# Reordering an attention-plus-feed-forward kernel: sink scores one pair later, one more x tile transposed by DMA

## The chip, the cores and the metric

The kernel runs on one core of a Trainium2 chip. The metric is the device time of one execution in microseconds (us); of several runs the median is taken. Before the change it is 197.56 us, the median of 8 runs between 197.08 and 198.56.

## What is computed

The reference takes q, k and v of 4 batches, 8 heads, 768 positions and 64 values per head, and five feed-forward inputs. First it does attention with a window and sinks:

```
scores = q @ k.T / sqrt(64)
keep   = (key position < 4) or (0 <= query position - key position < 128)
a      = softmax(where(keep, scores, -1e9))
attn   = a @ v
```

The heads of a position are laid side by side, which gives x with 3072 rows and 512 columns. Then comes a multiplicative feed-forward:

```
a = x @ w1        # 512 -> 1024
b = x @ w2        # 512 -> 1024
h = (a * b) @ w3  # 1024 -> 1024
out = h @ w_out   # 1024 -> 512
```

All inputs and the output are float32.

## The kernel before

**Tiles.** A batch b has three tiles t of 256 positions, and four pairs r of heads. The names of the plan (line 526 on) are steps of TensorE work, and each is one generator in the code:

- `t3.i.j` and `fm.i.n` fold w3 and w_out into one matrix `w3o` = w3 @ w_out: `t3` transposes a block of 128 rows of w3 (`fold_w3`), `fm` multiplies it with 128 columns of w_out (`fold_mm`). Blocks 0, 1 and 2 of w3 come as float32 on SyncE's (SP's) queue, in two halves; the other five come as bf16 on GpSimd's (POOL's) queue.
- `tpk`/`tpq.b.t` transpose k and q on TensorE. For the tiles in `XPOSE` the same is done by a DMA transpose from SP (`transposes_dma`, line 270).
- `sc.b.r.t` are the scores of a pair in a tile, then an exponential on ScalarE and the mask on VectorE (`scores`). One of them per batch or tile also makes the sink scores: four matmuls into the tile `sp` (line 303) and one exponential into `es`.
- `av.b.r.t` multiplies the weights with v and divides by their sum on VectorE (`values`); the result is the bf16 tile `xn`. `sv.b` makes the sink values.
- `xt.b.r.t` transposes x of two pairs on TensorE and copies it from PSUM to `xT` (`x_transposes`, line 360). For the tiles in `X_XPOSE` two DMA transposes from SP do this for a tile (`x_transposes_dma`, line 370), one for each 128 positions.
- `g.b.c.dt.half` is one half of a gate: half 0 is x @ w1 for 128 of the 1024 columns and chunk c of tokens, copied by ScalarE to `a_sb`; half 1 is x @ w2, multiplied with `a_sb` by VectorE into `ab`. Batch 0 has three chunks of 256 tokens; the others have two of 384. So g.2.1 needs x of tiles 1 and 2.
- `p.b.m` is the projection of 128 tokens with `w3o`, eight matmuls of 512 columns, copied out of PSUM and stored from SP.

**Order.** Nothing is scheduled at run time. The long loop at the end of the kernel plays the program through with estimated durations. It takes TensorE's work strictly in the order of `PLAN`. For the other engines (ScalarE, VectorE, SP) it puts each ready instruction in their order as the estimates say, so constants such as `LAG`, `SW_BEGIN`, the additions to `arrive`, `XX_US` and `XP_US` decide how SP's transposes and stores stand, which of ScalarE and VectorE copies out of PSUM, and where idle matmuls (`keep_busy`, tile `pz`) are put in a planned gap. On the chip every engine works through its own fixed list and waits for semaphores.

**Queues.** POOL issues the loads, with a cast from float32 to bf16, in the order of the list `order`; eight are in flight. SP issues the three float32 blocks of w3, then all DMA transposes and the stores, in one list, and a DMA of SP also waits until the one eight places before it has landed. PSUM has four buffers `mm` and two `sc`.

Of the kernel before, what the change touches and what calls it, by code (L numbers as in the profile page):

```python
# [21 lines left out]
def kernel(  # L22
# [29 lines left out]

    CHUNKS = [[(256 * i, 256 * i + 256) for i in range(3)]] + [[(0, 384), (384, 768)]] * (B - 1)
    XPOSE = [(1, 2), (2, 0), (2, 1), (2, 2), (3, 0), (3, 1), (3, 2)]
    X_XPOSE = [(2, 0), (2, 1), (2, 2), (3, 0), (3, 1), (3, 2)]
    CUTS = (0, 128, 256, 384, 512)
    HALVED = 8
    PIECES = ((0, 256), (256, 384), (384, 512))
# [1 line left out]
    SPLIT = (0, 1)  # L60
    RAW = (('w3', 0), ('w3', 1), ('w3', 2))
# [62 lines left out]
    def load(what, *i):  # L124
# [18 lines left out]
        else:  # L143
# [2 lines left out]


    RAW_US = 0.6
    order = [("w3", 5), ("wo", 128, 256), ("wo", 384, 512), ("w3", 4), ("wo", 0, 128), ("k", 0, 0), ("q", 0, 0),
             ("w3", 3), ("k", 0, 1), ("wo", 256, 384), ("v", 0, 0), ("q", 0, 1), ("w3", 7), ("w3",  # L150
             6), ("w2", 256, 512), ("q", 0, 2), ("v", 0, 1), ("w1", 256, 512), ("k", 0, 2), ("w2",
             768, 1024), ("w1", 768, 1024), ("w2", 512, 768), ("w1", 512, 768), ("w2", 0, 256),
             ("w1", 0, 256), ("v", 0, 2)] + [
             ("qkv", b, 0, 6) for b in range(1, B)]

    nc.scalar.preload_act_table_set("natural_log_exp_and_others")
# [302 lines left out]


    arrive = {}
    LAG, RATE, BEGIN, SW_BEGIN = (0.9, 2.5), 0.383, 2.0, 2.6

    def pieces(what, *i):
        if what == "qkv":
# [15 lines left out]
        else:  # L481
            yield 1.03 * (i[1] - i[0]) / 512, 1024, [(what, n) for n in range(i[0] // P, i[1] // P)]

    streams = [[[0.8 + RAW_US * n + 1.2, {"w3": 0.475, "wo": 1.03 * (CUTS[x[1] + 1] - CUTS[x[1]]) / 256 if x[0] == "wo" else 0}.get(x[0], 0.555),
                 {"w3": 4096, "wo": 4 * (CUTS[x[1] + 1] - CUTS[x[1]]) if x[0] == "wo" else 0}.get(x[0], 512), [("raw",) + x]] for n, x in enumerate(RAW)],
               [[None, mb, size, keys] for x in order for mb, size, keys in pieces(*x)]]
    at, issue, landed, heads_ = BEGIN, 1.3, [], [0, 0]
    STEP = 0.05
    issued = 0

    def issue_more():
        nonlocal issue, issued
        while issued < len(streams[1]) and (issued < 8 or len(landed) > issued - 8):
            if issued >= 8:
                issue = max(issue, landed[issued - 8])
            issue += {2: 0.6, 6: 1.25, 8: 0.9}.get(issued, 0.0)
            streams[1][issued][0] = max(SW_BEGIN, issue + 1.3)
            issue += 0.57 if streams[1][issued][2] == 4096 else 0.9
            issued += 1

    issue_more()
    while any(h < len(s) for h, s in zip(heads_, streams)):
        live = [n for n in (0, 1) if heads_[n] < len(streams[n])
                and streams[n][heads_[n]][0] is not None and streams[n][heads_[n]][0] <= at]
        total = sum(streams[n][heads_[n]][2] for n in live)
        for n in live:
            x = streams[n][heads_[n]]
            x[1] -= RATE * STEP * x[2] / total
            if x[1] <= 1e-9:
                heads_[n] += 1  # L510
                for key in x[3]:
                    arrive[key] = at + STEP + LAG[n] + (0.5 if at > 20.0 else 0.0)
                if n == 1:
                    landed.append(at + STEP + LAG[n])
                    issue_more()
        at += STEP

    for key in arrive:
        if key[0] in ("k", "q", "v"):
            arrive[key] += (0.0, 0.3, -0.5, 2.0)[key[1]]  # L520

    tasks = {}
    SP_US = 0.7
    XP_US, XX_US, LATE_US = (0.0, 9.0, 8.7, 7.8), (9.0, 9.0, 9.0, 7.7, 6.0, 3.6, 3.6, 3.6, 3.6), 12.0
    PLAN = """
        t3.0.0 t3.2.4 t3.0.4 t3.5.0 t3.2.0 t3.1.0 t3.1.4 fm.5.1 fm.2.1 fm.0.1 fm.1.1 fm.5.3 fm.0.3
        t3.4.0 fm.1.3 fm.2.3 fm.2.0 fm.0.0 fm.5.0 fm.4.0 fm.4.1 fm.1.0 tpk.0.0.2 tpq.0.0.0 tpk.0.0.0
        tpq.0.0.2 fm.4.3 t3.3.0 sc.0.0.0 sc.0.1.0 tpk.0.1.2 tpk.0.1.0 fm.3.0 fm.3.3 fm.1.2 fm.0.2 fm.3.2
        fm.5.2 sv.0 sc.0.2.0 av.0.0.0 av.0.1.0 fm.3.1 fm.2.2 sc.0.3.0 tpq.0.1.2 tpq.0.1.0 fm.4.2 t3.7.0
        xt.0.0.0 av.0.2.0 sc.0.0.1 sc.0.1.1 av.0.3.0 t3.6.0 fm.7.0 fm.7.1 fm.7.2 xt.0.2.0 fm.6.3 fm.7.3  # L530
        sc.0.2.1 sc.0.3.1 tpq.0.2.2 fm.6.1 av.0.0.1 av.0.1.1 fm.6.0 g.0.0.2.0 g.0.0.3.0 fm.6.2 tpk.0.2.0
        tpq.0.2.0 tpk.0.2.2 g.0.0.2.1 av.0.2.1 av.0.3.1 xt.0.0.1 sc.0.0.2 sc.0.1.2 g.0.0.6.0 g.0.0.7.0
        xt.0.2.1 g.0.0.7.1 g.0.0.6.1 g.0.0.3.1 g.0.1.7.0 g.0.1.7.1 g.0.0.4.0 sc.0.2.2 sc.0.3.2 g.0.0.4.1
        g.0.1.0.0 g.0.1.4.0 g.0.1.2.0 g.0.1.0.1 av.0.0.2 g.0.1.4.1 g.0.0.5.0 g.0.0.1.0 g.0.0.1.1
        g.0.1.2.1 g.0.0.5.1 av.0.1.2 g.0.1.5.0 g.0.0.0.0 tpk.1.0 xt.0.0.2 g.0.1.5.1 tpq.1.0 av.0.2.2
        g.0.0.0.1 g.0.1.3.0 av.0.3.2 sc.1.0.0 sc.1.1.0 sv.1 g.0.1.3.1 g.0.1.6.0 g.0.1.1.0 g.0.1.6.1
        tpk.1.1 g.0.1.1.1 xt.0.2.2 sc.1.2.0 sc.1.3.0 av.1.0.0 tpq.1.1 p.0.0 g.0.2.7.0 g.0.2.2.0 av.1.1.0
        g.0.2.6.0 g.0.2.6.1 sc.1.0.1 sc.1.1.1 av.1.2.0 av.1.3.0 g.0.2.2.1 g.0.2.7.1 p.0.1 g.0.2.0.0
        g.0.2.0.1 sc.1.2.1 sc.1.3.1 xt.1.2.0 g.0.2.5.0 g.0.2.1.0 g.0.2.5.1 av.1.0.1 g.0.2.3.0 av.1.1.1
        g.0.2.1.1 g.0.2.4.0 g.0.2.4.1 p.0.2 g.0.2.3.1 av.1.2.1 av.1.3.1 xt.1.0.0 p.0.3 xt.1.2.1 xt.1.0.1  # L540
        sc.1.0.2 sc.1.1.2 p.0.4 g.1.0.2.0 g.1.0.4.0 sc.1.2.2 sc.1.3.2 g.1.0.2.1 g.1.0.3.0 av.1.0.2
        g.1.0.5.0 g.1.0.4.1 av.1.1.2 g.1.0.7.0 av.1.2.2 g.1.0.5.1 av.1.3.2 g.1.0.7.1 g.1.0.3.1 g.1.0.6.0
        xt.1.0.2 xt.1.2.2 g.1.0.1.0 sc.2.0.0 sc.2.1.0 g.1.0.6.1 g.1.1.2.0 g.1.1.7.0 g.1.0.1.1 g.1.1.5.0
        g.1.1.7.1 g.1.1.2.1 av.2.0.0 sc.2.2.0 sc.2.3.0 av.2.1.0 g.1.1.5.1 g.1.1.4.0 g.1.1.4.1 g.1.1.1.0
        av.2.2.0 g.1.1.1.1 g.1.1.6.0 g.1.1.6.1 g.1.1.3.0 g.1.0.0.0 g.1.1.0.0 av.2.3.0 sc.2.0.1 sc.2.1.1
        g.1.1.3.1 sv.2 p.0.5 g.1.1.0.1 g.1.0.0.1 sc.2.2.1 sc.2.3.1 av.2.0.1 p.1.4 av.2.1.1 sc.2.0.2
        sc.2.1.2 av.2.2.1 av.2.3.1 p.1.5 sc.2.2.2 sc.2.3.2 p.1.3 av.2.0.2 av.2.1.2 sc.3.0.0 sc.3.1.0
        av.2.2.2 p.1.2 p.1.0 av.2.3.2 sc.3.2.0 sc.3.3.0 p.1.1 g.2.0.1.0 g.2.0.7.0 g.2.0.2.0 av.3.0.0
        g.2.0.1.1 g.2.0.7.1 g.2.0.2.1 av.3.1.0 g.2.0.5.0 g.2.0.4.0 g.2.0.5.1 g.2.0.0.0 g.2.0.0.1
        g.2.1.4.0 av.3.2.0 g.2.0.4.1 g.2.1.0.0 g.2.1.3.0 g.2.1.4.1 g.2.1.3.1 g.2.1.5.0 g.2.1.0.1  # L550
        g.2.1.1.0 g.2.0.3.0 sv.3 g.2.1.5.1 av.3.3.0 g.2.1.2.0 sc.3.0.1 sc.3.1.1 g.2.0.3.1 g.2.1.1.1
        g.2.0.6.0 g.2.0.6.1 g.2.1.2.1 g.2.1.6.0 sc.3.2.1 sc.3.3.1 av.3.0.1 av.3.1.1 p.2.0 sc.3.0.2
        sc.3.1.2 av.3.2.1 av.3.3.1 p.2.2 g.2.1.7.0 sc.3.2.2 sc.3.3.2 g.2.1.7.1 av.3.0.2 g.2.1.6.1 p.2.1
        av.3.1.2 p.2.5 av.3.2.2 p.2.3 g.3.0.6.0 g.3.0.5.0 av.3.3.2 g.3.0.1.0 g.3.0.5.1 g.3.0.6.1
        g.3.0.4.0 g.3.0.1.1 g.3.0.4.1 g.3.0.2.0 g.3.0.3.0 g.3.0.0.0 g.3.0.0.1 g.3.0.2.1 p.2.4 g.3.1.6.0
        g.3.1.6.1 g.3.0.3.1 g.3.1.7.0 g.3.1.2.0 g.3.1.0.0 g.3.1.2.1 g.3.1.7.1 g.3.1.0.1 g.3.1.4.0
        g.3.1.3.0 g.3.1.1.0 g.3.1.4.1 g.3.0.7.0 g.3.0.7.1 g.3.1.1.1 g.3.1.3.1 p.3.0 g.3.1.5.0 g.3.1.5.1
        p.3.1 p.3.2 p.3.4 p.3.3 p.3.5
    """

    def task(name, prio, gen, stages, after=(), loads=(), ring=None, started=(),
# [25 lines left out]
    for i in range(KFF):  # L587
        t3 = []
# [16 lines left out]
    def xn_free(b, t):  # L605
        b, t = (b, t - 2) if t == 2 else (b - 1, t + 1)
        return [] if b < 0 else ([("xd", b, t, i) for i in range(2)] if (b, t) in X_XPOSE else
                                 [("xt", b, r, t) for r in (0, 2)])

    unit = []  # L610
    for b in range(B):
        for t in range(NT):
# [32 lines left out]
            for r in range(NP):  # L645
# [2 lines left out]
                    after.append(("g", b - 2, len(CHUNKS[b - 2]) - 1, KFF - 1, 1))  # L648
                lead = r % 2 == 0
                sinks = None  # L650
                if t > 0 and r == 0 and (b in SPLIT or t == 1):
                    sinks = (t, t + 1) if b in SPLIT else (1, NT)
                    after.append(("sk", b))
                    if b not in SPLIT:
                        after += [("tdq", b, 4), ("tdq", b, 5)] if (b, 2) in XPOSE else [("tpq", b, 2)]
# [7 lines left out]
                     + ([("av",) + unit[-3]] if lead and len(unit) > 3 else []))  # L663
                task(("av", b, r, t), 3, values(b, r, t),
                     [("pe", 0.181 if t == 0 else 0.357), ("dve", 0.6)],
                     [("sc", b, r, t)] + ([("sv", b)] if t else []) + (xn_free(b, t) if r == 0 else []),
                     [("v", b, kb) for kb in kbs], "mm",
                     [("av",) + unit[-1]] if unit else [])
                unit.append((b, r, t))
# [129 lines left out]
    with tc.manual_schedule(engines={mybir.EngineType.PE, mybir.EngineType.Activation,  # L799
                                     mybir.EngineType.DVE, mybir.EngineType.SP}):  # L800
        while len(done) < len(tasks):
            for k in tasks.values():
                e, us = k["stages"][0]
                if e != "pe" and k["name"] not in begun and all(a in done for a in k["after"] + k["late"]):
                    begun.add(k["name"])
                    k["stage"] = 0
                    at = max([arrive[x] for x in k["loads"]] + [done[a] for a in k["after"]]
                             + [done[a] + LATE_US for a in k["late"]])
# [77 lines left out]
```

## Time and profile before

| | |
|---|---|
| median of 8 runs | 197.56 us (197.08 to 198.56) |
| the profiled execution's own time | 197.25 us |
| its span, first to last instruction | 195.6 us |
| TensorE busy | 189.7 us, 97% of the span |
| VectorE, ScalarE, GpSimd busy | 116.8, 103.5, 73.7 us |
| granted TensorE clock | 1.0 |
| moved by DMA | 27.32 MB, mean 140 GB/s |
| DMA transposes on SP's queue | 40: 14 of k, 14 of q, 12 of x |

The page shows for each engine its busy time and then 40 slices of the span, each a digit of tenths. A chain of waits goes back from the last instruction to whatever released it. In a line of instructions, `L383` is the line of the kernel, `pg<-xT,w_sb` the written and read tiles, `x36` the count. Landing times of single loads are read from the trace's issue and completion of each DMA.

### The profile page before, as it was taken

To read this page: it belongs to the slowest core of one execution; us is meant where nothing else is said; L and a number is where in the kernel's file an instruction comes from. 1 tells how busy PE (TensorE), PEld (TensorE's weight loads), DVE (VectorE), ACT (ScalarE), POOL (GpSimd) and SP (SyncE) were. 2 spreads that over 40 slices of the span, in tenths; PEclk is the share of its full clock that TensorE was granted. 3 is DMA by queue.
4 is the path that set the end of the run, shared out by engine and by line. 5 is a ranking of instruction groups with operands and counts; after the bars stand their busy time and mean duration, and the time that the engine had idled before them with its cause. 6 is when DMAs were issued, how large, how long until landed. Compare 5 with 4: busy or idle time off the path is not lost.

```text
span 195.6 us, 4901 instructions
## 1 busy us (share of the span) xinstructions
PE 189.7 (97%) x1985; PEld 127.6 (65%) x1996; DVE 116.8 (60%) x282; ACT 103.5 (53%) x185; POOL 73.7 (38%) x98
## 2 busy tenths in 40 slices
PE   7999999999999999999999999999999999999993
PEld 2599889889877775675665564656555556555443
DVE  5065798878887762786757866645576624254212
ACT  2244788785477636817556775332767443323210
POOL 7993756669999731536655100000000000000000
PEclk9999999999999999999999999999999999999999
DMA  6999999999999999999999999990312242010134
GB/s 210 245 188 189 181 188 183 196 176 155 156 152 130 157 185 128 211 185 150 153 143 149 168 173 171 264 181 0 29 29 80 84 160 56 0 57 0 54 124 144
DMA packets 103702, 27.32 MB, mean 140 GB/s; under 512 B 95232, under 2 KB 99712, under 8 KB 103680
## 3 DMA queue, kind: packets, MB, share of 16 engines
q0 software_dynamic: 77744, 13.90, 93.0%
q1 hardware_dynamic: 25792, 13.05, 34.6%
q8 instruction: 15, 0.25, 0.5%
q10 hardware_dynamic: 144, 0.07, 0.1%
q14 instruction: 7, 0.06, 0.1%
HBM read 29.36 MB, written 6.29 MB: 182 GB/s over the span
## 4 chain that ended last, share of the span: by engine, by line
PE 89%; DMA 7%; SPq 1%; ACT 1%; issue 1%; DVE 0%
PE pg L383 39%; PE po L423 19%; PE av L343 8%; PE pw L413 8%; PE sc L309 6%; DMA xT<-xn 4%; DMA ab<-in_moe_w_dram 3%; PE tp L402 2%; PE tp L261 2%; PE xt L360 1%; PE tp L233 1%; PE po L440 1%; PE sp L303 1%; PE vp L284 0%; ACT ex L317 0%
## 5 line engine op out<-in xcount | busy, mean ns | idle before, releaser
L383 PE MATMUL pg<-xT,w_sb 128*128 128x384 bf16 (+1 forms) x576 | 91.0, 308 | 0.4 <-DMA xT<-xn 0.4
L383 PEld LDWEIGHTS <-w_sb 128*128 128x128 bf16 x576 | 54.0, 98 | 27.7 <-issue 1.8
L387 DVE TENSOR_TENSOR ab<-a_sb,pg 128x384 bf16<-128x384 f32 (+1 forms) x72 | 36.3, 508 | 31.1 <-PE pg L383 26.6
L390 ACT COPY a_sb<-pg 128x384 f32<-128x384 f32 (+1 forms) x72 | 32.0, 444 | 37.7 <-PE pg L383 26.8
L317 ACT ACTIVATE ex<-sc 128x1024 bf16<-128x1024 f32 (+1 forms) x48 | 43.9, 955 | 5.4 <-PE sc L309 5.2
L423 PE MATMUL po<-w3o,ab 128*128 128x512 bf16 x173 | 42.3, 379 | 0.6
L321 DVE TENSOR_TENSOR am<-ex,maskt 128x1024 bf16<-128x1024 bf16 (+1 forms) x48 | 29.7, 640 | 1.9 <-ACT ex L317 1.7
L423 PEld LDWEIGHTS <-ab 128*128 128x128 bf16 x184 | 17.2, 98 | 18.5 <-issue 0.5
L226 ACT COPY o_sb<-po 128x512 f32<-128x512 f32 x18 | 10.6, 586 | 25.6 <-PE po L423 25.6
L350 DVE TENSOR_TENSOR xn<-av,rec 128x256 bf16<-128x256 f32 x48 | 20.4, 425 | 1.7
L115 POOL DMA_DIRECT2D qN<-in_q_dram x18 | 15.9, 885 | 9.8 <-DMA vN<-in_v_dram 6.2
L115 POOL DMA_DIRECT2D vN<-in_v_dram x18 | 15.9, 886 | 9.6 <-DMA kN<-in_k_dram 8.0
L343 PE MATMUL av<-vN,am 128*128 128x65 bf16 x352 | 19.3, 193 | 0.0
L343 PEld LDWEIGHTS <-am 128*128 128x128 bf16 x352 | 16.7, 97 | 2.8 <-issue 0.6
L115 POOL DMA_DIRECT2D kN<-in_k_dram x18 | 15.9, 883 | 6.2 <-DMA qN<-in_q_dram 5.3
L347 DVE RECIPROCAL rec<-av 128x4 f32<-128x4 f32 x48 | 8.5, 178 | 14.1 <-PE av L343 13.8
L413 PE MATMUL pw<-wo_sb,w3t 128*128 128x128 bf16 x256 | 16.1, 219 | 0.0
L413 PEld LDWEIGHTS <-w3t 128*128 128x128 bf16 x256 | 14.6, 98 | 0.4
L309 PE MATMUL sc<-qT,kT 64*128 64x128 bf16 (+1 forms) x256 | 14.1, 238 | 0.0
L343 PE MATMUL av<-vs,es 128*128 128x130 bf16 x64 | 12.5, 221 | 0.0
L309 PEld LDWEIGHTS <-kT 64*128 64x128 bf16 x256 | 8.2, 94 | 5.0 <-issue 3.6
L226 DVE COPY o_sb<-po 128x512 f32<-128x512 f32 x5 | 3.5, 692 | 8.7 <-PE po L423 8.6
(70 smaller groups left out, 127.2 us busy)
## 6 DMA issues: line engine op xcount, KB each, us to landing
out_dram<-o_sb SPq DMA_DIRECT2D x23, 256.0 KB, 5.8
vN<-in_v_dram POOLq DMA_DIRECT2D x24, 128.0 KB, 10.2
kN<-in_k_dram POOLq DMA_DIRECT2D x18, 128.0 KB, 11.1
qN<-in_q_dram POOLq DMA_DIRECT2D x18, 128.0 KB, 11.4
w_sb<-in_moe_w_dram POOLq DMA_DIRECT2D x8, 256.0 KB, 9.8
ab<-in_moe_w_dram SPq DMA_DIRECT2D x3, 512.0 KB, 4.3
ab<-in_moe_w_dram POOLq DMA_DIRECT2D x5, 256.0 KB, 9.0
wo_sb<-in_moe_w_out_dram POOLq DMA_DIRECT2D x4, 256.0 KB, 8.2
```

The source lines that it names most:

```text
L115: nc.gpsimd.dma_start(out=dst, in_=rows(src, b, kb))
L226: (nc.scalar.copy if home[me] == "act" else nc.vector.tensor_copy)(dst, src)
L309: nc.tensor.matmul(sc[:, e, c:c + n], kT[b][hp, r, kb * P:(kb + 1) * P], qT[b][hp, r, qb * P:qb * P + n], start=True, stop=True)
L317: nc.scalar.activation(ex[:, :, c0:], sc[:, :, c0:], ACTF.Exp, scale=scale)
L321: nc.vector.tensor_mul(am[:, :, c0:], ex[:, :, c0:], mk)
L343: nc.tensor.matmul(o, lhs, rhs, start=(n == 0), stop=(n == len(todo) - 1), skip_group_check=True)
L350: nc.vector.tensor_mul(xns[b, t][:, :, r, :, :], av[:, :, :, 0:D], rec[:].to_broadcast([P, 2, 2, D]))
L383: nc.tensor.matmul(pg[:], w_sb[:, kk, dt * P:(dt + 1) * P], xT[b][:, kk, tk], start=(kk == 0), stop=(kk == NP - 1))
L387: nc.vector.tensor_mul(ab[b][:, dt, tk], gate_a.pop((b, c, dt))[:], pg[:])
L390: nc.scalar.copy(a_sb[:], pg[:])
L413: nc.tensor.matmul(po[:], w3T[i][:, j, :], wo_sb[:, j, n0:n1], start=(j == 0), stop=(j == KFF - 1))
L423: nc.tensor.matmul(po[:], ab[b][:, kk, m * P:(m + 1) * P], w3o[:, kk, :], start=(kk == 0), stop=(kk == KFF - 1))
```

## The change

- `X_XPOSE` gets (1, 2): x of batch 1's tile 2 is transposed by two DMA transposes from SP in place of `xt.1.0.2` and `xt.1.2.2` on TensorE.
- In batches 2 and 3 the sink scores of tiles 1 and 2 are made with pair r = 2 of tile 1, where they were made with r = 0; the `av` of pairs 0 and 1 of tile 1 then also wait for that step.
- The list `order` of loads up to batch 0's end is another one; its first five are w3, w3, w_out, w_out, w_out.
- The constants of the estimated landings are others, and an addition `LATER` for each batch and block of 128 positions takes the place of one for each batch.
- `PLAN` is another order of the same steps, without the two `xt`. The matmuls are the same apart from these, except that six idle ones are left of sixteen.

```diff
-    X_XPOSE = [(2, 0), (2, 1), (2, 2), (3, 0), (3, 1), (3, 2)]
+    X_XPOSE = [(1, 2), (2, 0), (2, 1), (2, 2), (3, 0), (3, 1), (3, 2)]
...
-    order = [("w3", 5), ("wo", 128, 256), ("wo", 384, 512), ("w3", 4), ("wo", 0, 128), ("k", 0, 0), ("q", 0, 0),
...
+    order = [("w3", 3), ("w3", 4), ("wo", 0, 128), ("wo", 256, 384), ("wo", 384, 512), ("w3", 7), ("q", 0, 0),
+             ("k", 0, 0), ("w3", 6), ("wo", 128, 256), ("k", 0, 1), ("v", 0, 0), ("q", 0, 1), ("q",
...
-    LAG, RATE, BEGIN, SW_BEGIN = (0.9, 2.5), 0.383, 2.0, 2.6
+    LAG, RATE, BEGIN, SW_BEGIN = (0.55, 1.0), 0.383, 2.4, 1.6 + 0.97 * len(RAW)
...
+    LATER = ((0.0,) * 6, (0.0,) * 6, (-4.0, -4.0, -2.0, 0.0, 1.0, 1.0), (3.0, 3.0, 3.0, 2.5, 3.5, 7.0))
     for key in arrive:
         if key[0] in ("k", "q", "v"):
-            arrive[key] += (0.0, 0.3, -0.5, 2.0)[key[1]]
+            arrive[key] += LATER[key[1]][key[2]]
...
-    XP_US, XX_US, LATE_US = (0.0, 9.0, 8.7, 7.8), (9.0, 9.0, 9.0, 7.7, 6.0, 3.6, 3.6, 3.6, 3.6), 12.0
+    XP_US, XX_US, LATE_US = (0.0, 8.0, 8.3, 7.5), (9.0, 9.0, 9.0, 7.5, 7.5, 4.5, 3.5, 3.5, 3.5), 12.0
...
-                if t > 0 and r == 0 and (b in SPLIT or t == 1):
+                if (t > 0 and r == 0) if b in SPLIT else (t == 1 and r == 2):
...
-                     [("sc", b, r, t)] + ([("sv", b)] if t else []) + (xn_free(b, t) if r == 0 else []),
+                     [("sc", b, r, t)] + ([("sv", b)] if t else [])
+                     + ([("sc", b, 2, 1)] if t == 1 and r < 2 and b not in SPLIT else []) + (xn_free(b, t) if r == 0 else []),
```

The part of the plan around batch 2's last tile, before:

```
sc.2.2.2 sc.2.3.2 p.1.3 av.2.0.2 av.2.1.2 sc.3.0.0 sc.3.1.0 av.2.2.2 p.1.2 p.1.0
av.2.3.2 sc.3.2.0 sc.3.3.0 p.1.1 g.2.0.1.0 g.2.0.7.0 g.2.0.2.0 av.3.0.0 g.2.0.1.1
g.2.0.7.1 g.2.0.2.1 av.3.1.0 g.2.0.5.0 g.2.0.4.0 g.2.0.5.1 g.2.0.0.0 g.2.0.0.1 g.2.1.4.0
```

and after:

```
sc.2.2.2 sc.2.3.2 p.1.3 p.1.5 sc.3.0.0 sc.3.1.0 av.2.2.2 av.2.3.2 p.1.4 sc.3.2.0
sc.3.3.0 p.1.0 g.2.0.5.0 g.2.0.1.0 g.2.0.5.1 g.2.0.4.0 g.2.0.1.1 av.3.0.0 g.2.0.0.0
g.2.0.7.0 g.2.0.7.1 g.2.0.4.1 g.2.1.7.0
```

## The prediction

> **What bounds the kernel now.** I read the page's busy table and slices first, then TensorE's waits, then the chain of waits around the one wait that lies in mid kernel. Busy share and slices:
>
> ```profile
> PE 189.7 (97%) x1985; PEld 127.6 (65%) x1996; DVE 116.8 (60%) x282; ACT 103.5 (53%) x185; POOL 73.7 (38%) x98
> ...
> PE   7999999999999999999999999999999999999993
> ...
> DMA  6999999999999999999999999990312242010134
> ```
>
> TensorE (PE) is full from slice 2 to slice 39, so the time is the sum of its matmuls plus its waits. But the DMA engines are full too, from slice 2 to slice 27 (4.9 us a slice: until 132 us). These two bounds run side by side for two thirds of the kernel, and what a change of order is worth is decided where they touch. TensorE's waits, in total, name the touch:
>
> ```profile
> PE pz L458 <- DVE ksbd L180: 1.3, 1, 1.3
> PE tp L402 <- DMA ab<-in_moe_w_dram: 0.4, 1, 0.4
> PE pg L383 <- DMA xT<-xn: 0.4, 1, 0.4
> ```
>
> The chain of waits (start us, length, what) shows where that last one is:
>
> ```profile
> 120.19 0.36 PE av L343 x10
> 120.54 0.29 PE sc L309 x4
> ...
> 123.14 7.42 DMA xT<-xn
> 130.56 0.14 issue
> 130.69 0.81 PE pg L383 x4
> ```
>
> At 130.69 TensorE enters the second token half of batch 2's gates (g.2.1), which needs x of batch 2's last tile, transposed by DMA. The plan asked for it at 130.3; it landed at 130.56. SyncE's (SP's) issue timeline before it has hardly a pause:
>
> ```profile
> 111.23 1.24 SPq L270 DMA_TRANSPOSE kT<-kN  x1
> 112.56 3.81 SPq L370 DMA_TRANSPOSE xT<-xn  x2
> 116.47 1.01 SPq L430 DMA_DIRECT2D out_dram<-o_sb  x2
> 117.57 1.35 SPq L270 DMA_TRANSPOSE qT<-qN  x1
> 119.01 1.22 SPq L270 DMA_TRANSPOSE kT<-kN  x1
> 120.36 0.97 SPq L430 DMA_DIRECT2D out_dram<-o_sb  x2
> 121.88 3.21 SPq L370 DMA_TRANSPOSE xT<-xn  x2
> ```
>
> So this transfer sits at the end of a full issue queue and of full DMA engines. It took 7.42 us, where the fastest of its kind in this trace takes 2.3.
>
> **The change, part by part.**
>
> *x of batch 1's tile 2 by DMA.* Removed: eight transposes of batch 1 on TensorE (in the chain 0.45 us at 87.71) and two PSUM copies on engines that are not the bound. Gain 0.45 us of TensorE. Added: two DMA transposes on SP's queue, 1.2 to 1.6 us of issue each by the rows above, and DMA work: with nothing behind them, landings at the end of the stretch follow each other by 0.5 us (131.49, 132.00, 132.48), in the crowd by about 1.0. So +1.0 to +2.0 us on engines that are full until 132. Their reader, g.1.1, is covered: between av.1.3.2 and g.1.1.5.0 the new plan has 15 gate halves (0.65 each), four av (0.18), two pairs of scores (0.44 and 0.55) and one projection (1.73), 13.2 us, against 0.6 (VectorE) + about 2.8 (two issues) + 6.2 to 7.4. (These durations, and those below, are the chain's: a gate half is four matmuls, 36 in 5.85 us at 131.69; a projection eight, 1.73 at 107.56.) Without that cover it would cost the difference, some 2 us at most.
>
> *Sink scores of batches 2 and 3 a pair later.* Nothing is removed: the same four matmuls (0.33 us) and one exponential, for r = 2 instead of r = 0; four av wait for it. It gives qT of the last tile 1 to 2 us more. That tile was read 1.4 us after landing (100.27, 101.67). With two more transposes ahead, landing moves to 101.3 to 102.1; the new plan asks near 102.3. I take 0, bounds 0 to +0.5.
>
> *Load order and the first microseconds.* Before, TensorE ran sixteen idle matmuls (pz), waited, and started real work at 8.29:
>
> ```profile
> 8.29 2.86 PE L402 MATMUL tp<-ident,ab 128*128 128x128 f32 x28 [0.44 <-DMA ab<-in_moe_w_dram]
> 10.99 0.39 PE L413 MATMUL pw<-wo_sb,w3t 128*128 128x128 bf16 x4
> ```
>
> From 10.99 it never waited again until 130.69. The POOL queue landed 7.86 (w3), 9.60 (wo), 11.03 (wo), 12.26 (w3), 13.78 (wo): 1.2 us after a w3, 1.4 to 1.7 after a wo. The new order is w3, w3, wo, wo, wo: 7.86, 9.1 to 9.6, 10.5 to 11.0. The new plan does six raw halves and two w3 blocks, then its first fold product, which needs the third load: it starts at 10.6 to 11.1, having done one w3 block (eight transposes of 0.056, 0.45 us) more. Lead: 0.45 + 10.99 − 11.05 = 0.4 us (bounds 0.3 to 0.85). Six pz are left of sixteen, so three gaps (about 0.8, 0.4, 1.0 us, estimated from these landings) stand open between 7 and 11 us. Afterwards most loads are asked for within about a microsecond of landing; I allow 0 to 0.8 us of small waits up to 60 us and take 0.3.
>
> Here a rule of the Trainium skill speaks against the change ("TensorE: Matmul & The Clock Gate", Part 1): an idle activity window of about 3.4 us drops the array to half clock, and it needs about as long to come back. The row above is the test: after 0.44 us of quiet ahead of 8.29 the bf16 transposes still ran at 0.056 us each and the granted clock is full throughout. No new gap alone is near 3.4 us, so by the row I charge 0; by the rule, should the broken-up stretch count as idle, half speed for 3.4 us is +1.7 us, most of it hidden later (below).
>
> *The new plan.* I count what stands before and after the touch. Ahead of av.2.3.2 it has one projection less (10 for 11; 1.73 us) and the two xt less. av.2.3.2 began at 120.19, so now at 120.19 − 1.73 − 0.45 − 0.4 + 0.3 = 117.9, ending 118.3. Then come two projections (3.46), two scores (0.44), nine gate halves (5.85), one av (0.18): TensorE asks for g.2.1 at 118.3 + 9.93 = 128.2. (The same count for before: 120.55 + 0.44 + 1.73 + 7.15 + 0.36 = 130.2, as traced.) Behind g.2.1's start, before took 192.49 − 130.69 = 61.80 us with no wait; the new plan has two gate halves and one av more there: 61.80 + 1.30 + 0.18 = 63.28.
>
> *When does x of batch 2's tile 2 land?* **Lower bound**: it follows its producer as before, 120.55 to 130.56, 10.0 us: 128.3, no wait. **Upper bound**: the queue decides. By the built program, SP has the same nine transposes of batch 3 ahead of it, one output less, and two x transposes more; outputs landed 0.65 apart (127.51, 128.16). Full engines: 130.56 + 2 × 0.5 to 2 × 1.0 − 0.65 = 130.9 to 131.9. That bound also lets POOL's loads finish first; a transpose that is issued sooner overtakes some of them (from 100 to 125 us both queues land in turn). Two outputs and three transposes of batch 3 stand close in front, so SP reaches the pair at about 121.5 and ends its issue at 123 to 124; issue end to landing was 5.5 to 6.9 us from 100 to 130 us. That is 128.5 to 130.9. I take **130.4**, nearer the queue's side, because the DMA row is full in every slice up to there.
>
> A second rule weighed against the row: the skill's "DMA: Bandwidth & Descriptors" ("Latency and other measured facts") gives a transfer from SP's queue about 0.6 us to its first byte and a transpose 261 GB/s, which for the 128 KB of one 128 x 512 block is 0.5 us (an estimate; the unloaded landings 0.5 us apart agree). By that alone the pair lands under 2 us after its issue, before 126, and there is no wait: rival 1's 196.4. The row, 7.42 us from issue to landing on loaded engines, decides.
>
> **Sum.** Wait 130.4 − 128.2 = 2.2 us, taking the place of 0.4. End of TensorE's chain: 130.4 + 0.13 + 63.28 = 193.81 against 192.49: +1.32 us. The profiled execution took 197.25 (span 195.6 and 1.65 around it); the median of the runs is 0.31 above it. 197.25 + 1.32 + 0.31 = **198.9 us**.
>
> **Rivals.**
>
> 1. *The transfer keeps pace with its producer (faster).* SP is free when x is ready, the pair lands by 128.3. Then all gains stand: lead 0.4, eight transposes 0.45, the old wait 0.4, less 0.3: 0.95 to 1.25 off, 196.3 to 196.6. For it: in the trace SP issues this pair 0.7 us after xn is written (121.2, 121.88). Against: the full issue rows above, with two transposes more in them. It decides when the pair's issue ends before 122.3.
> 2. *A wash.* Landing between 128.6 and 129.6: 197.1 to 198.1.
> 3. *More waits than one.* The gaps at 7 to 11 us cool the clock, or g.2.0 (its x landed at 122.60 and was read at 122.65) waits too and pushes what follows. Delays before 118 move av.2.3.2 with them, so they are hidden only in part: 200.2 to 202. Against it: those waits end before the one at g.2.1 and come out of the same slack.
>
> **How the numbers follow.** Forecast (landing 129.7 to 131.9, 198.2 to 200.4): 0.55. Rival 1: 0.18. Rival 2: 0.15. Rival 3: 0.12. The runs of before spread 0.3% about their median, so 0.3% (0.6 us) is what can be told from no change: faster, below 197.0, 0.18; same 0.16; slower, above 198.15, 0.66. The range 196.3 to 200.4 cuts off rival 3 and the lower edge of rival 1. Alone, the forecast has 198.2 to 200.4.
>
> **What would show it.** Right: in TensorE's waits, pg L383 on DMA xT with about 2 us near 130 us (here 0.4); xt L360 with 40 matmuls for 48; xT by DMA x14; first fold product near 11 us; six pz; the end of the DMA row still at 132 us or later. Wrong: no such wait and the next gate at 128; small waits on ab, wo or w_sb that add up to over 1 us before 60 us; a granted clock below full after 8 us; or 0.05 us steps doubling after 11 us.

## The result

The changed kernel takes **200.03 us** (median of 11 runs, 198.13 to 201.06) against 197.56: the ratio is 1.0111, with a 95% interval of 1.0085 to 1.0137. It is slower by 2.2 us by the ratio, by 2.5 us by the medians. The profiled execution took 200.71 us, its span 199.0. Here and below a ratio leaves out runs more than 1.5% above the fastest of their kernel: seven runs in four of the experiments, all with a mean granted clock of 0.990 or 0.991.

The page's slices, of the changed kernel:

```profile
PE   6699999999999999999999999769999999999993
...
PEclk9999999999999999999999999969999999999999
DMA  6999999999999999999999999990022331010134
```

From slice 3 on TensorE is full again but for slices 26 and 27, and in slice 27 its granted clock has a dent that the kernel before did not have. DMA is full to the same slice, which now ends at 134 us. TensorE's waits:

```profile
PE pg L383 <- DMA xT<-xn: 2.9, 1, 2.9
PE tp L402 <- DMA ab<-in_moe_w_dram: 1.4, 2, 1.2
...
PE tp L402 <- DVE w3t L226: 0.8, 1, 0.8
PE pw L413 <- DMA wo_sb<-in_moe_w_out_dram: 0.4, 1, 0.4
```

The one wait on xT has grown from 0.4 to 2.9 us; the other waits shown end by 11.00 us, where the first fold product starts. The chain of waits around it (start, length, what):

```profile
117.44 0.82 PE av L343 x20
118.26 1.51 PE po L423 x7
...
123.18 7.37 DMA xT<-xn
130.54 0.64 issue
131.18 3.71 PE pg L383 x12
134.89 0.21 PE vp L284
```

The last av of batch 2 ends at 118.26 and TensorE asks for g.2.1 at 128.3. The two x transposes are issued from 123.18 and land at 130.54 and 131.09. Then twelve gate matmuls of 384 columns take 3.71 us, where the same number took 1.95 at 85.76 us of the kernel before, at full clock. SP's issue timeline shows why the pair starts so late:

```profile
107.05 0.54 SPq L430 DMA_DIRECT2D out_dram<-o_sb  x1
110.10 1.20 SPq L270 DMA_TRANSPOSE kT<-kN  x1
112.01 1.19 SPq L270 DMA_TRANSPOSE qT<-qN  x1
113.29 2.91 SPq L370 DMA_TRANSPOSE xT<-xn  x2
116.30 2.51 SPq L270 DMA_TRANSPOSE kT<-kN  x1
118.90 1.37 SPq L270 DMA_TRANSPOSE qT<-qN  x1
120.40 0.49 SPq L430 DMA_DIRECT2D out_dram<-o_sb  x1
121.00 1.21 SPq L270 DMA_TRANSPOSE kT<-kN  x1
122.73 0.34 SPq L430 DMA_DIRECT2D out_dram<-o_sb  x1
123.18 2.55 SPq L370 DMA_TRANSPOSE xT<-xn  x2
```

From 107.6 to 110.1 SP stands still: the next transpose needs k of batch 3's block 2, which landed at 110.08 (103.81 before). Everything behind it in the list moves with it, and x, complete at 119.1, is issued 4.1 us later (0.7 us before). Two shifts make up this difference: x is complete 2.1 us sooner than before (119.1 for 121.2), and SP reaches it 1.3 us later (123.18 for 121.88).

Last, the stretches of 3.41 us around the wait (length, TensorE busy, granted clock, DMA share, GB/s):

```profile
127.64:131.06 3.42, 0.65 (x4) 1.00 1.30 221
131.06:134.47 3.41, 3.29 (x11) 0.50 0.95 194
134.47:137.88 3.41, 3.41 (x35) 1.00 0.00 0
```

After a stretch in which TensorE was busy for 0.65 of 3.42 us, one whole stretch is granted at half clock. Its 3.29 us of work would have been about 1.65 at full clock, half of it. The mean granted clock of a run tells whether it had such a stretch, since 3.41 us at half clock in 199 us make 0.991. Six of the eleven runs show 0.991, and they took 200.03 to 201.06 us; the other five show 0.999 or 1.0 and took 198.13 to 199.59.

### The profile page after: what moved, and what is told of

Its sections match the earlier page's. It is cut to its first block, busy times and chain, and to the rows that moved or that the text cites. A ratio compares the mean times of both kernels' runs of the same rounds, so it can differ in the third digit from the quotient of the medians.

```text
span 199.0 us, 4856 instructions
## 1 busy us (share of the span) xinstructions
PE 188.3 (95%) x1965; PEld 126.7 (64%) x1978; DVE 117.4 (59%) x284; ACT 101.8 (51%) x181; POOL 73.9 (37%) x98
## 4 chain that ended last, share of the span: by engine, by line
PE 87%; DMA 8%; DVE 1%; issue 1%; POOL 1%; ACT 0%; POOLq 0%; DVEq 0%
PE pg L383 40%; PE po L423 20%; PE pw L413 8%; PE av L343 7%; PE sc L309 6%; DMA wo_sb<-in_moe_w_out_dram 4%; DMA xT<-xn 4%; PE tp L261 2%; PE xt L360 1%; PE tp L233 1%; PE po L440 1%; PE sp L303 1%; PE tp L402 1%; POOL ab L131 1%; PE vp L284 0%
## 5 line engine op out<-in xcount | busy, mean ns | idle before, releaser
L383 PEld LDWEIGHTS <-w_sb 128*128 128x128 bf16 x576 | 54.9, 99 | 31.9 <-DMA xT<-xn 3.2
L423 PE MATMUL po<-w3o,ab 128*128 128x512 bf16 x171 | 41.3, 379 | 0.7 <-DVE xn L350 0.2
L321 DVE TENSOR_TENSOR am<-ex,maskt 128x1024 bf16<-128x1024 bf16 (+1 forms) x48 | 30.2, 641 | 3.2 <-ACT ex L317 3.0
L226 ACT COPY o_sb<-po 128x512 f32<-128x512 f32 x17 | 10.0, 586 | 23.4 <-PE po L423 21.4
L343 PE MATMUL av<-vN,am 128*128 128x65 bf16 x352 | 18.6, 193 | 0.0
L226 DVE COPY o_sb<-po 128x512 f32<-128x512 f32 x6 | 4.2, 692 | 9.8 <-PE po L423 9.8
## 6 DMA issues: line engine op xcount, KB each, us to landing
vN<-in_v_dram POOLq DMA_DIRECT2D x24, 128.0 KB, 10.8
```

The lines of the kernel that those rows point to most:

```text
L226: (nc.scalar.copy if home[me] == "act" else nc.vector.tensor_copy)(dst, src)
L321: nc.vector.tensor_mul(am[:, :, c0:], ex[:, :, c0:], mk)
L343: nc.tensor.matmul(o, lhs, rhs, start=(n == 0), stop=(n == len(todo) - 1), skip_group_check=True)
L383: nc.tensor.matmul(pg[:], w_sb[:, kk, dt * P:(dt + 1) * P], xT[b][:, kk, tk], start=(kk == 0), stop=(kk == NP - 1))
L423: nc.tensor.matmul(po[:], ab[b][:, kk, m * P:(m + 1) * P], w3o[:, kk, :], start=(kk == 0), stop=(kk == KFF - 1))
```

## The experiments

The theory after the result has three terms: the plan asks for x of batch 2's last tile before SP's list and the DMA engines can bring it (**the wait**); the quiet of that wait lowers the clock (**the clock**); what makes the transfer late is SP's in-order list, or the amount of DMA work, or both (**the transfer**). The rival is that the time goes all along the kernel, in early gaps and small waits.

**Ask later.** Gates of batch 2's first half go ahead of g.2.1.

```diff
-g.2.0.4.1 g.2.1.7.0 g.2.1.7.1 g.2.0.0.1 sv.3 av.3.1.0 sc.3.0.1 sc.3.1.1 g.2.0.2.0 g.2.0.2.1 g.2.0.6.0 g.2.0.6.1
+g.2.0.4.1 g.2.0.0.1 sv.3 av.3.1.0 g.2.0.2.0 g.2.0.2.1 g.2.0.6.0 g.2.0.6.1 sc.3.0.1 sc.3.1.1 g.2.1.7.0 g.2.1.7.1
```

> The changed kernel with four gate halves of g.2.0 (2.6 us) and g.2.0.0.1, sv.3, av.3.1.0 and one pair of scores put ahead of g.2.1.7.0, so that TensorE asks for x of batch 2's last tile some 4.4 us later; nothing else moves. Theory (the plan asks too early for a transfer that the DMA side sets): the pair lands at 131 as before the edit, the wait of 2.9 us falls to 0 and with it the 3.4 us at half clock behind it; 195.5 to 196.5 us, 3.5 to 4.5 below the changed kernel and 1 to 2 below the kernel before. Rival (the time is lost all along, in the early gaps and in small waits): the wait goes, but no more than 1 us is won, 199 us.

Measured: 196.16 us (12 runs, 196.02 to 197.56), ratio to the kernel before 0.9925 (0.9906 to 0.9945). The pair still lands at 130.10 and 130.87. The chain runs through that time on TensorE alone:

```profile
127.22 3.25 PE pg L383 x20
130.47 0.21 PE vp L284
130.68 0.18 PE av L343 x6
130.86 2.60 PE pg L383 x16
133.47 0.55 PE sc L309 x12
```

The half gates of g.2.1 start behind these scores, at 134.01, when the pair has long landed. (This execution is one of two in twelve that took 197.5 us; it lost about 1.5 us ahead of this place, to a half-clock stretch at 8.7 us that is shown below.) So the wait and its clock were the whole loss, and more: 3.9 us come back by the medians, 3.7 by the ratios, by moving a few names in the plan. The rival falls. This is also the fastest version: by the ratio 0.75% or 1.5 us below the kernel before.

**Fill the wait.** Twelve idle matmuls stand in the wait.

```diff
-g.2.0.4.1 g.2.1.7.0
+g.2.0.4.1 pz.0 g.2.1.7.0      # pz.0: 12 idle matmuls, 128 x 512
```

> The changed kernel with twelve idle 512-column matmuls (2.6 us) ahead of g.2.1.7.0, in the wait. The wait itself stays. If half clock after the wait is a cost of its own, the granted clock stays full from 131 us and the time falls by 1.4 to 1.7 us in the runs that had it: median 198.4 and less spread than 198.1 to 201.1. If the clock costs nothing, or the idle matmuls delay the gates, 200.0 to 200.5.

Measured: 198.73 us (198.69 to 199.04), ratio 1.0055 (1.0036 to 1.0073). Its chain:

```profile
128.30 2.59 PE pz L458 x12
130.89 0.23 issue
131.12 2.11 PE pg L383 x12
```

The gate starts at 131.12, as it did without the idle matmuls (131.18), so the wait is the same. But the twelve gate matmuls take 2.11 us for 3.71, and the granted clock is full from 5.4 us to the end of TensorE's work. The clock is a cost of its own: 1.6 us in these two executions, 1.3 us of the median. All six runs have a mean granted clock of 0.998 or more and lie within 0.35 us, against 2.9 in the changed kernel. Not all of this is the clock. The five runs of the changed kernel at full clock still differ by 1.5 us, and the idle matmuls end at 130.89, so that a pair that lands sooner than that gains nothing here.

**Fill part of it.** The same with six matmuls, and with three.

> The changed kernel with six idle matmuls (1.3 us) at the start of the wait instead of twelve: 1.6 us of quiet are left of 2.9. If the clock drops only for a window of 3.4 us that is almost wholly quiet, it holds in every run: median 198.6 to 198.9, no run above 199.3. If quiet of half a window is enough, some runs are at 200 and more, as in the changed kernel.

> The changed kernel with three idle matmuls (0.65 us) at the start of the wait: 2.2 us of quiet are left. If a window must be quiet for about 80% (2.8 of 3.4 us, as in the changed kernel's profiled run), it holds: 198.6 to 199.0. If two thirds are enough, the runs split into about 198.7 and about 200.3.

Measured: with six 198.73 us (14 runs, 198.14 to 201.37, one of them above 199.2), ratio 1.0039 (1.0022 to 1.0056); with three 199.18 (9 runs, 198.26 to 201.43, four of them at 199.8 or more), ratio 1.0065 (1.0039 to 1.0091). The mean granted clock of each run says which of them had a half-clock stretch (it does not say where):

| idle matmuls in the wait | runs at 0.991 | their times |
|---|---|---|
| none | 6 of 11 | 200.03 to 201.06 |
| three | 1 of 9 | 201.43 |
| six | 2 of 14 | 198.70, 201.37 |
| twelve | 0 of 6 | |

So with any of these fillings the drop is rare (3 of 29 runs, against 6 of 11), and three are not seen to be worse than six. The three runs of 199.80 to 199.85 with three idle matmuls have a clock of 1.0: what made them longer is not the clock, and stays open. The profile with three is the run of 201.43. There the pair landed at 131.90, the quiet after the idle matmuls was 3.0 us and not 2.2, and the next stretch was at half clock:

```profile
128.29:131.70 3.41, 0.62 (x3) 1.00 1.27 224
131.70:135.11 3.41, 3.12 (x10) 0.50 1.42 180
```

With six the median was as expected, but one run lies above 199.3. With three neither reading is borne out: the times do split, but not by the clock.

**SP's order.** The batch 3 transposes of blocks 3 to 5 wait in SP's list until the pair has gone.

```diff
-                             war + (extra.get("tp" + n, []) if b == 1 else []), [(n, b, kb)],
+                             war + (extra.get("tp" + n, []) if b == 1 else [])
+                             + ([("av", 2, NP - 1, 2)] if b == 3 and kb > 2 else []), [(n, b, kb)],
```

> The changed kernel with the k and q transposes of batch 3's blocks 3 to 5 behind the pair of x transposes of batch 2's last tile in SyncE's queue. Same transfers, same plan on TensorE. Theory A (SyncE's in-order queue holds the pair 4 us after its x is written at 119.1): the pair issues by 120.5, lands near 127.5 to 128.5, the wait is under 0.6 us; a new one of about 1 us can come at the scores of batch 3; 196.5 to 198 us. Theory B (the DMA engines are full, whatever the order): the pair still lands at 130 or later, the wait stays above 1.5 us, 199.5 to 200.5.

Measured: 197.05 us (22 runs, 196.20 to 199.69), ratio 0.9961 (0.9942 to 0.9979). The pair is issued at 119.27 and lands at 126.86 and 128.37. SP's list, in part:

```profile
107.73 0.53 SPq L430 DMA_DIRECT2D out_dram<-o_sb  x1
111.14 1.20 SPq L270 DMA_TRANSPOSE kT<-kN  x1
...
119.27 2.54 SPq L370 DMA_TRANSPOSE xT<-xn  x2
```

The wait at g.2.1 is gone from TensorE's list, and the expected new one is there:

```profile
PE tp L402 <- DMA ab<-in_moe_w_dram: 2.2, 3, 1.3
PE sc L309 <- DMA qT<-qN: 1.7, 1, 1.7
```

Theory A holds: with the same transfers on equally full engines, the order of SP's list alone moves the landing by 2.7 us. SP still stands for k of batch 3's block 2 (2.8 us, until 111.14), so the room comes from the moved entries, three of which stood ahead of the pair (116.30, 118.90 and 121.00 in the changed kernel), and not from an end of that wait.

**One part undone: x of batch 1's last tile on TensorE.**

```diff
-    X_XPOSE = [(1, 2), (2, 0), (2, 1), (2, 2), (3, 0), (3, 1), (3, 2)]
+    X_XPOSE = [(2, 0), (2, 1), (2, 2), (3, 0), (3, 1), (3, 2)]
...
-sc.2.2.0 sc.2.3.0 g.1.0.3.0
+sc.2.2.0 sc.2.3.0 xt.1.0.2 xt.1.2.2 g.1.0.3.0
```

> The changed kernel with x of batch 1's last tile back on TensorE (X_XPOSE without (1, 2), the two xt behind sc.2.3.0 in the plan): one part of the change undone. It gives back 0.45 us of TensorE work and takes two transposes out of SyncE's queue and 1 to 2 us of DMA work from ahead of batch 3's loads. Theory (those two transposes make the pair late): the pair lands 1 to 2 us sooner in relation to its x, the wait falls below 1.5 us, and the time by 1 to 2 us, to 198 to 199. Rival (the order of the rest does it): wait 2.4 us or more, time 199.7 to 200.3.

Measured: 197.72 us (22 runs, 196.63 to 200.79), ratio 0.9987 (0.9965 to 1.0008). The time is under the 198 to 199 that were expected; five of the runs, four of them at 199.7 or more, still had a half-clock stretch (0.990 or 0.991). In the profiled execution the wait at g.2.1 is 0.46 us, partly because TensorE asks 0.65 us later (128.94 for 128.29). SP issues the pair at 122.82, hardly sooner than in the changed kernel (123.18), but it lands at 128.85 and 129.31. DMA issues of that pair alone (count, median us from issue to landing), here and then in the changed kernel:

```profile
xT<-xn SPq DMA_TRANSPOSE x2, 5.6
```

```profile
xT<-xn SPq DMA_TRANSPOSE x2, 7.0
```

POOL's last load landed at 126.53 here and at 130.73 there. So the amount of DMA work counts as well: without the two transposes k of batch 3's block 2 lands at 105.06 for 110.08, and the pair 1.8 us sooner. One thing is not separated here: SP's list of this kernel, built by the same estimates, also has batch 3's k and q in another order.

**The same part undone where nothing waits.** The kernel that asks later, with those eight transposes on TensorE.

> The kernel that asks later, with x of batch 1's last tile transposed on TensorE. There is no wait at g.2.1 in either, so what is left is the price of eight transposes on TensorE: 0.45 us slower than with the DMA, 196.5 to 196.7 (median). Rival: the two DMA transposes cost as much elsewhere as they save, 196.0 to 196.3.

Measured: 196.75 us (14 runs, 196.60 to 197.09), ratio 0.9948 (0.9930 to 0.9965), by the medians 0.59 us above the version with the DMA, by the two ratios 0.45. The saving is real once nothing waits for the DMA side.

**The part alone in the kernel before**, its plan without the two xt and nothing else moved.

```diff
-    X_XPOSE = [(2, 0), (2, 1), (2, 2), (3, 0), (3, 1), (3, 2)]
+    X_XPOSE = [(1, 2), (2, 0), (2, 1), (2, 2), (3, 0), (3, 1), (3, 2)]
...
-xt.1.0.2 xt.1.2.2 g.1.0.1.0
+g.1.0.1.0
```

> The kernel before, with this one part of the change alone: x of batch 1's last tile by DMA and its two xt out of the plan, nothing else moved. In this plan only five gate halves and one pair of scores (3.7 us) lie between the last av of batch 1 and the first g.1.1. Theory (the transfer takes 10 to 11 us from av to landing and is worth nothing without cover): TensorE waits 6 to 7 us near 90 to 96 us, partly given back by the wait at g.2.1; 202 to 204 us. Rival (the transfer is short, as its bytes say): wait under 2 us, 197 to 199 us.

Measured: 205.12 us (4 runs), ratio 1.0371 (1.0325 to 1.0418). The wait, and then stretches of the clock's length around it:

```profile
PE pg L383 <- DMA xT<-xn: 7.7, 1, 7.7
```

```profile
87.92:91.34 3.42, 1.66 (x15) 1.00 2.31 156
91.34:94.75 3.41, 0.00 (x0) 1.00 1.90 143
94.75:98.16 3.41, 0.87 (x3) 0.50 1.74 156
98.16:101.58 3.42, 3.42 (x12) 0.50 1.89 156
```

The transfer is worth nothing without cover. Wait and time lie above what was expected (6 to 7 us, 202 to 204): the two stretches at half clock, with 4.29 us of work in them, add some 2.1 us, half of that work. The rows also tell more of the clock: a stretch that was half busy (1.66 us) was followed by full clock, an empty one by half clock, and a half-clock stretch with 0.87 us of work by another.

**The other part undone: sink scores on pair 0.**

```diff
-                if (t > 0 and r == 0) if b in SPLIT else (t == 1 and r == 2):
+                if t > 0 and r == 0 and (b in SPLIT or t == 1):
...
-                     + ([("sc", b, 2, 1)] if t == 1 and r < 2 and b not in SPLIT else []) + (xn_free(b, t) if r == 0 else []),
+                     + (xn_free(b, t) if r == 0 else []),
```

> The changed kernel with the sink scores of batches 2 and 3 back on pair 0 of tile 1, and the av of tile 1 free of that wait. The plan asks for q of batch 2's last tile one pair of scores and some gates sooner. Theory (that tile lands near 102 us): TensorE waits 5 to 8 us for qT before 104 us, and the wait at g.2.1 goes; 203 to 205 us. Rival (q of that tile lands in time either way): no such wait, 199.5 to 200.5 us.

Measured: 205.63 us (4 runs), ratio 1.0397 (1.0346 to 1.0448).

```profile
PE sp L303 <- issue: 7.1, 1, 7.1
```

TensorE stands for 7.1 us ahead of the sink scores until 101.68, and q of batch 2's last block lands at 101.59. The time is again above what was expected (203 to 205), and again two stretches at half clock lie in and behind the wait (97.79 to 104.62, with 2.72 us of work). In the rest of this plan, moving the sink scores by a pair hides that wait.

**The early gaps.** The profiled execution of the kernel that asks later took 197.56 us where ten of its twelve runs took 196.0 to 196.2. Its stretches:

```profile
5.29:8.70 3.41, 1.36 (x12) 1.00 1.05 270
8.70:12.12 3.42, 3.35 (x24) 0.50 1.77 178
```

TensorE was busy for 1.36 us of the first stretch, with a wait of 2.1 us for the first bf16 block of w3 in it, and the next was granted at half clock. The two runs at 197.5 have a mean granted clock of 0.991, the ten others 0.998 or more, so it is the clock that sets these two apart. So ten more idle matmuls were put into the three gaps.

```diff
-t3.1.0 t3.3.0 t3.2.4 t3.2.0 t3.4.0 fm.1.0
+t3.1.0 pz.0 t3.3.0 pz.1 t3.2.4 t3.2.0 t3.4.0 pz.2 fm.1.0      # 5, 3 and 2 idle matmuls
```

> The kernel of the experiment that asks later for x of batch 2's last tile, with ten more idle matmuls (five, three and two) in the three gaps between 7 and 11 us. If the early gaps let the clock drop in some runs (3.4 us at half speed from 8.7 us in that kernel's profiled run, 197.5 us in two of its twelve), no run is above 196.8 and the median is 196.0 to 196.3. If that drop had another cause, some runs stay near 197.5; if the idle matmuls delay the loads' users, the median rises by up to 0.5.

Measured: 196.34 us (9 runs, 196.24 to 197.18), ratio 0.9941 (0.9916 to 0.9967). No run shows less than 0.998, but one is at 197.18, and the rest take 196.24 to 196.73, against 196.02 to 196.22 of the good runs without them. That the idle matmuls keep the clock up is not shown: two in twelve without them is too few to tell, and the kernel that asks later with x back on TensorE, which has no such matmuls either, shows no run under 0.998 in fourteen. As a cure they gain nothing.

## Why the prediction was right

The direction, the place and the mechanism were right, and the time lies in the range; the likeliest value was 1.1 us low. There is luck in the number. The five runs at full clock have a median of 198.79, which is the forecast's 198.9, and the six with a half-clock stretch one of 200.92, above the range's 200.4; the median of all eleven, 200.03, is the fastest of those six. Two of the signs of being wrong that the prediction named did show: a granted clock below full after 8 us, and waits on ab and wo of over 1 us ahead of 60 us (1.4 and 0.4), though these are the gaps ahead of 11 us that it had counted. Step by step, on the profiled execution:

| step | predicted | measured |
|---|---|---|
| first fold product | 11.05 | 11.00 |
| end of av.2.3.2 | 118.3 | 118.26 |
| TensorE asks for g.2.1 | 128.2 | 128.3 |
| the pair of x transposes has landed | 130.4 | 131.09 |
| wait at g.2.1 | 2.2 | 2.89 |
| from there to the end of TensorE's chain | 63.28 | 64.85 |
| end of the chain, against before | +1.32 | +3.54 |

The first and the last of these, in the chain of the changed kernel:

```profile
11.00 5.21 PE pw L413 x88
...
194.25 1.78 PE po L440 x24
```

*The walk along the plan* held to 0.1 us up to the wait. That is in part luck: the 0.3 us allowed for small waits was not needed up to 60 us, where none shows after 11 us, but as much went afterwards. From 60 to 118 us TensorE stood for 0.57 us, from 60 to 120 before for 0.32. The lead of 0.4 us is read from the trace; no run has the new order of loads alone.

*The landing* was 0.7 us late of the estimate. SP reached the pair at 123.18 and not at about 121.5, and the time from the end of the issue (125.73) to the landing, 5.4 us, was no longer than allowed. So the issue was the term that was too small. The estimate counted what stands ahead of the pair in SP's list, and not what these entries wait for themselves: SP stood for 2.5 us for k of batch 3's block 2, which landed 6 us later than before. That this wait is what was missing is read from the trace and not shown, since no run takes it away. The two experiments on the transfer show both halves of the estimate to count, the order of SP's list (2.7 us of landing) and the DMA work of the two transposes (1.8 us of landing at nearly the same issue).

*The clock* was the step that failed. It was charged 0 because no gap was near 3.4 us, and the price of a drop was said to be mostly hidden later. The drop came at the wait itself, where nothing behind hides it, and took 64.85 − 63.28 = 1.57 us. The row that I had gone by, 0.44 us of quiet with no effect, said nothing of a wait of 2.2 us, which the same prediction derives further down. The Trainium skill's rule ("TensorE: Matmul & The Clock Gate", Part 1) was nearer, though by its words an idle window is needed, and here windows with 0.65 and 1.36 us of work were enough.

The sum closes: +1.32 predicted, +0.65 for the later restart (131.18 for 130.53), +1.57 for the clock make 3.54. It is the sum of the profiled execution. The median lies 0.7 us below that, among the runs with a drop; the runs without one take 2.1 us less than those with it (198.79 and 200.92), which is more than the 1.57, so that they probably waited less too. No profile of such a run is there to show it.

*x by DMA*: gain 0.45, measured 0.45 to 0.59 where nothing waits. The cover of g.1.1 held, no wait shows there. But "some 2 us at most" for a missing cover was far off, and does not follow from the prediction's own terms: 9.6 to 10.8 us from av to landing less 3.7 us of cover are 5.9 to 7.1. Measured was a wait of 7.7 us. *Sink scores*: no wait shows, as taken; what the move is worth in this plan, a wait of 7.1 us, was not seen.

*The rivals.* The first, a transfer that keeps pace with its producer, did not come about here, but with SP's list reordered it did, at 197.05, above that rival's 196.3 to 196.6 since another wait of 1.7 us came up. Its own condition, an issue that ends before 122.3, fits both (121.8 there, 125.7 here). The one of several waits had a part of the truth, the clock, in another place.

## What to carry to other kernels

When a plan is packed until TensorE never waits, a change of order is judged at the one place where the plan meets the transfer side: count the work from the producer to the request, and follow the transfer through its issuing queue, entry by entry, with what each entry itself waits for. Moving the request by a few independent steps may be worth more than any work saved. Price a wait of some 2 us or more (2.1 and 2.9 us here) with the clock drop that can follow it, and look for the drop in the granted clock of every run, not in the times alone.

## What was not expected of the hardware

- The granted clock changes on a grid of 3.41 us: in the changed kernel at 4.76, 131.06 and 134.47 us, which are 37 and 1 times 3.413 apart (idle matmuls took 0.46 us each ahead of 4.76, and 0.22 where they were put into the wait at 128 us), and elsewhere half clock lasted 3.41 us (8.70 to 12.12) or twice that (94.75 to 101.58). Stretches with 0.65 of 3.42 and 1.36 of 3.41 us of TensorE work were followed by half clock, one with 1.66 of 3.42 by full clock. How a wait falls on the grid differs from run to run (in these profiles full clock begins between 4.50 and 7.30 us), which fits that only six of the eleven runs had the drop.
- With two more transposes of 128 KB a load came 5.0 us later (110.08 against 105.06 without them), and the loads of batch 3 from k of block 2 on 4 to 8 us later than in the kernel before, though the second of a pair lands only 0.55 us after the first (130.54 and 131.09). What multiplies it, the turns between the two queues or POOL's limit of eight loads in flight, stays open: no run separates these, nor the order of SP's list from them.
